# One stationary of 128 columns for V's high and low parts, in an attention and feed-forward kernel on one core

## The chip, the core and the metric

The kernel runs on one core of a Trainium2 chip. A core has a matrix engine (TensorE, PE in the profile, with its weight loads shown as PEld), a vector engine (VectorE, DVE), a scalar engine (ScalarE, ACT), a general engine (GpSimd, POOL), a queue engine (SyncE, SP) and 16 DMA engines. Matrix products land in PSUM, everything else works in SBUF. The metric is the device time of one execution in microseconds, lower is better. Before the change the median of three runs is 987.06 us (986.11 to 989.94).

## The reference

```python
# attention: B, H, S, D = 4, 8, 768, 64, 16 centroids per head, all float32
q_assign = argmax(q_n . c_n);  k_assign = argmax(k_n . c_n)      # cluster of each token
mask = q_assign[:, :, :, None] == k_assign[:, :, None, :]
scores = where(mask, q @ k.T / sqrt(D), -1e9)
attn = exp(scores - max);  attn = attn / (sum(attn) + 1e-9)
x = (attn @ v)                                  # (B, H, S, D), then to (B*S, H*D) = (3072, 512)
# feed forward: d_model 512, d_ff 2048
h = x @ w_in
g = h * tanh(softplus(h))                       # mish
out = g @ w_out
```

The result is to have float32 accuracy. The matrix engine is fed with pairs of 16-bit numbers, a high part and a low part (the rest), and products of parts are added up in PSUM.

## The kernel before

Attention is cut into 96 units: batch and head outermost (32 of them, called g), and inside each head three blocks `qb` of 256 queries. A unit has two halves `a` of 128 queries. For each half PE makes the scores (L488 and L493, float32), DVE takes the row maximum (L503), ACT the exponential (L510), POOL or DVE the reciprocal of the sum (L520, L521), POOL the high part of the normalized probabilities (L539) and DVE the low part (L556), both 16 bit; a DMA transposes both into the tile `pt`, whose 12 slices of keys are six of the high part and six of the low part (L572). This is what the units after batch 0 do. In batch 0 (units 0 to 23, where `mode` is 3) the probabilities stay float32, PE transposes them (L549), and V is float32 too.

Two units are one product with V, `pv(m)`. After batch 0 it has three parts: high of V times high of p, low of V times high of p, high of V times low of p. Each part takes six slices of 128 keys, and in each slice there is one matmul for either unit: a stationary of 64 columns (the 64 columns of the head in V), 256 columns of `pt` moving. The first unit's matmuls write partitions 0 to 63 of the PSUM tile `o`, the second unit's partitions 64 to 127, turn by turn. So there are 3 x 6 x 2 = 36 matmuls in one `pv`, and 36 such products after batch 0. Then `pv_out` takes each unit's 64 x 256 numbers out of PSUM: ACT writes the high 16-bit part of `x` (L617), DVE the low part (L618).

The feed-forward part works on blocks of 256 tokens: `m1(j)` makes 256 rows of h for one block (24 matmuls, L649 to L651), `e_mish`, `e_gh` and `e_gl` (ACT L659, POOL L663, DVE L671) make the 16-bit parts of g, `m2(k, a, f)` adds g times w_out into the tile `O` (six matmuls a step, L687 to L689), `m_out` takes it out (ACT L695). It runs some 25 units behind attention, so that PE has both kinds of work from batch 1 on. Before that the weights are converted: `w_abs`, `w_f32`, `w_sq` (L239 to L264), then `w_hi` and `w_lo` (L282 to L297) split them in two parts.

The order is not written by hand. Every step is put into a plan with a due time, in units of attention, from the table `T` (L806): for instance `m2` says how many steps after its block's first m1 a block's second product is due, `w0` when the two halves of the weights start, `prep_hi` when q and k are prepared. Fractions such as `f_a`, `f_b` and `f_w` say which share of a step's runs goes to one engine rather than another. A scheduler then orders the instructions on each engine from the plan and the dependences, and every engine works its own list in that order. Buffers come from pools (`xp` holds the tiles of `x`, `mp` small tiles of the feed-forward part), and a PSUM bank called "M" is shared by `o`, the transposed one-hots `oh` and a few scalars.

Of the kernel before, what the change touches and what calls it, by code (L numbers as in the profile page):

```python
# [8 lines left out]
F32 = mybir.dt.float32  # L9
F32R = mybir.dt.float32r  # L10
F16 = mybir.dt.float16
# [3 lines left out]
AF = mybir.ActivationFunctionType  # L15
ALU = mybir.AluOpType
AX = mybir.AxisListType

B, H, S, D, NCL = 4, 8, 768, 64, 16
DM, DFF = 512, 2048  # L20
P = 128
BIG = float(2.0**64)
E20 = 485165195.40979
PS = float(2.0**14)
# [31 lines left out]
def tile_clustered_attention_mish_ffn(  # L56
# [9 lines left out]
    nc = tc.nc  # L66
    pool = lambda name, bufs, **kw: ctx.enter_context(tc.tile_pool(name=name, bufs=bufs, **kw))
# [4 lines left out]
    op1 = pool("operands1", 1)  # L72
# [2 lines left out]
    pp = pool("probs", 3)  # L75
    hlp = pool("probs16", 3)
    ptp = pool("probsT", 3)
    xp = pool("x", 21)
    mp = pool("moe", 2)
    gp = pool("g", 1)  # L80
    sm = pool("small", 4)
# [6 lines left out]
    def share(n, key, late):  # L88

        f = T[key, int(late)]  # L90
        return int((n + 1) * f) != int(n * f)
# [24 lines left out]
    units = [(g, qb, g) for g in range(NG) for qb in range(3)]  # L116
# [89 lines left out]
    st = {}  # L206
# [93 lines left out]
    vst = {}  # L300
# [222 lines left out]
    def mode(i, a):  # L523


        n, late = 2 * i + a, i >= T["units0"]
        if i < 3 * H:
            return 3
        return 2 if share(n, "f_lo", late) else int(share(n, "f_hi", late))
# [46 lines left out]
    def pv(m):  # L576

        for i in (2 * m, 2 * m + 1):
            b, h = divmod(units[i][0], H)
            pl.after(("ptrans", i, 0), ("ptrans", i, 1), ("v_split", b, h // 2))  # L580
        o = ps2.tile([P, 512], F32, tag="M", name=f"o{m}", bufs=1)
        parts = 1 if mode(2 * m, 0) == 3 else 3
        for part in range(parts):
            for c in range(6):
                for s in range(2):
                    b, h = divmod(units[2 * m + s][0], H)
                    v = vst[b, h // 2][:, c, h % 2]
                    nc.tensor.matmul(  # L588
                        o[s * D : s * D + D, :256],
                        v if parts == 1 else v[:, int(part == 1)],  # L590
                        st["pt", 2 * m + s][:, :, c + (6 if part == 2 else 0), :],
                        start=(part == 0 and c == 0), stop=(part == parts - 1 and c == 5), skip_group_check=True,
                    )
        if parts == 1:

            for s in range(2):
                for a in range(2):
                    pl.after(("recip", 2 * m + s, a))
                    c0 = 256 + a * P
                    nc.tensor.matmul(  # L600
                        o[s * D : s * D + D, c0 : c0 + P], st["l", 2 * m + s, a].to_broadcast([P, D]), ident,
                        start=True, stop=True, skip_group_check=True,
                    )
        st["o", m] = o

    def pv_out(i):
        pl.after(("pv", i // 2))
        g, qb, _ = units[i]
        b, h = divmod(g, H)
        r, r2 = i % 2 * D, h % 2 * D  # L610
        o = st["o", i // 2][r : r + D]
        if ("x", b, h // 2, qb) not in st:
            st["x", b, h // 2, qb] = xp.tile([P, 2, 256], F16, tag="x", name=f"x{b}_{h // 2}_{qb}")
        x = st["x", b, h // 2, qb]
        if mode(i, 0) != 3:
            x = x[r2 : r2 + D]
            nc.scalar.activation(x[:, 0], o[:, :256], AF.Copy, scale=1.0 / PS)  # L617
            nc.vector.scalar_tensor_tensor(  # L618
                x[:, 1], o[:, :256], 1.0 / PS, x[:, 0], op0=ALU.mult, op1=ALU.subtract
            )  # L620
            return
        if h % 2 == 0:
            st["xf", h // 2, qb] = hlp.tile([P, 256], F32, tag="hl", name=f"xf{h // 2}_{qb}")
        xf = st["xf", h // 2, qb]
        if i % 2 == 0:
            st["rb"] = mp.tile([P, 256], F32, tag="osb", name=f"rb{i}", bufs=1)
            nc.scalar.activation(st["rb"], st["o", i // 2][:, 256:], AF.Copy, scale=vst[b, "p"])
        nc.vector.tensor_tensor(xf[r2 : r2 + D], o[:, :256], st["rb"][r : r + D], op=ALU.mult)
        if h % 2:
            nc.scalar.copy(x[:, 0], xf)  # L630
            nc.gpsimd.tensor_tensor(x[:, 1], xf, x[:, 0], op=ALU.subtract)

# [97 lines left out]
    for n in range(32):  # L730
        p = n // 16
# [5 lines left out]
    for i in range(16):  # L737
        p = i // 8
# [35 lines left out]
    for i in range(NU):  # L774
        for a in range(2):
            pl.at(i + T["scores", a], scores, i, a)
            pl.at(i + T["rowmax", a], rowmax, i, a)
            pl.at(i + T["expo", a], expo, i, a)
            pl.at(i + T["recip", a], recip, i, a)
            q = "q" if mode(i, a) == 3 else "p"  # L780
            pl.at(i + T[f"{q}_hi", a], p_hi, i, a)
            pl.at(i + T[f"{q}_lo", a], p_lo, i, a)
            pl.at(i + T[f"{q}_trans", a], ptrans, i, a)
        if i % 2:
            pl.at(i + T["pv"], pv, i // 2)
            pl.at(i + T["pv_out"], pv_out, i - 1)
            pl.at(i + T["pv_out"], pv_out, i)
# [32 lines left out]
    ('dq', 'copy_z'): 0,  # L820
    ('dq', 'copy_b'): -9,
    ('dq', 'copy_a'): 0,
    ('f_copy_t', 0): 0.269,
    ('f_copy_z', 0): 0.567,
    ('f_copy_b', 0): 0,
    ('f_copy_a', 0): 0,
# [2 lines left out]
    ('f_copy_b', 1): 0,  # L829
    ('f_copy_a', 1): 0.193,  # L830
    ('f_a', 0): 1,
    ('f_a', 1): 0.582,
    ('f_b', 0): -1,
    ('f_b', 1): 0.674,
    'prep_hi': 3.0343,
    'prep_lo': 1.2726,
    'copy_t': 0.5952,
    'copy_z': 0.8008,
    'copy_b': 3.5728,
# [13 lines left out]
    ('q_lo', 1): 1.5418,  # L853
    ('q_trans', 1): 1.5,
    ('f_w', 0): 0,
    ('f_w', 1): 0.7,
    'lead': 0.5333,
    'units0': 24,
    ('f_d', 0): 0.965,
# [10 lines left out]
    ('span', 0): 1.1575,  # L870
    ('span', 1): 1.0762,
    ('load', 0): -3.8837,
    ('load', 1): 2.8855,
    ('w0', 0): 0.89,
    ('w0', 1): 9.386,
    ('w_d', 0): 0.3597,
    ('w_d', 1): 0.1964,
    ('ws0', 0): 4.1159,
# [7 lines left out]
    'put': 2.3669,  # L886
    ('scores', 0): 0.4,
    ('rowmax', 0): 0.9821,
    ('expo', 0): 1.3834,
    ('recip', 0): 0.7,  # L890
    ('scores', 1): 1.8591,
    ('rowmax', 1): 1.6368,
# [7 lines left out]
    ('p_trans', 1): 1.5,  # L900
    'pv': 3.4,
    'pv_out': 3.6,
    'm2': 3.759,
    'm_out': 0.4,
}

# [27 lines left out]
```

## Time and profile before

| what | value |
|---|---|
| median of three runs | 987.06 us (986.11 to 989.94) |
| the profiled execution: its own time | 990.56 us |
| its span in the trace | 988.8 us |
| PE busy | 913.1 us (92%) |
| PEld busy | 660.7 us (67%) |
| DVE, ACT, POOL busy | 652.6, 542.3, 425.6 us (66, 55, 43%) |
| granted TensorE clock, mean | 0.98 of full speed |

The profiled execution is 3.5 us above the median of the runs, and 1.8 us of its time lie outside the span. Busy time of PE is the union over overlapping matmuls: a matmul's own duration is longer than its distance to the next one, so distances between starts are the measure of what one costs.

### The profile page before, as it was taken

To read this page: it belongs to the slowest core of one execution; us is meant where nothing else is said; L and a number is where in the kernel's file an instruction comes from. 1 tells how busy PE (TensorE), PEld (TensorE's weight loads), DVE (VectorE), ACT (ScalarE), POOL (GpSimd) and SP (SyncE) were. 2 spreads that over 40 slices of the span, in tenths; PEclk is the share of its full clock that TensorE was granted. 3 is DMA by queue.
4 is the path that set the end of the run, shared out by engine and by line. 5 is a ranking of instruction groups with operands and counts; after the bars stand their busy time and mean duration, and the time that the engine had idled before them with its cause. 6 is when DMAs were issued, how large, how long until landed. Compare 5 with 4: busy or idle time off the path is not lost. (4 is left out here: it accounts for less than half of the span.)

```text
span 988.8 us, 17975 instructions
## 1 busy us (share of the span) xinstructions
PE 913.1 (92%) x6913; PEld 660.7 (67%) x6913; DVE 652.6 (66%) x1149; ACT 542.3 (55%) x898; POOL 425.6 (43%) x539
## 2 busy tenths in 40 slices
PE   3898688998998999999999999899999999999997
PEld 3666466676666766766777767667777777676764
DVE  6988985877867776867767777767776766211110
ACT  3777374775656666476656747556556565211111
POOL 3225785626535444653544544744444433111010
PEclk9999788999999999999999999999999999999999
DMA  9734623136785776667678766667667656100000
GB/s 360 238 78 149 183 60 69 45 79 130 132 158 97 163 126 115 134 142 152 122 147 144 149 135 127 125 131 139 132 114 136 120 106 115 43 12 22 12 11 22
DMA packets 250165, 115.50 MB, mean 117 GB/s; under 512 B 229600, under 2 KB 229600, under 8 KB 250080
## 3 DMA queue, kind: packets, MB, share of 16 engines
q1 hardware_dynamic: 238272, 82.50, 42.3%
q10 hardware_dynamic: 11808, 31.86, 11.4%
q8 instruction: 54, 0.88, 0.4%
q14 instruction: 31, 0.25, 0.1%
HBM read 35.68 MB, written 6.29 MB: 42 GB/s over the span
## 5 line engine op out<-in xcount | busy, mean ns | idle before, releaser
L510 ACT ACTIVATE p<-s,m 128x768 f32<-128x768 f32 x192 | 172.7, 900 | 161.3 <-DVE m L503 123.3
L649 PE MATMUL h<-x,w 128*128 128x256 f16 x768 | 210.0, 273 | 2.7 <-ACT u L659 1.8
L650 PE MATMUL h<-x,w 128*128 128x256 f16 x768 | 209.6, 273 | 0.3 <-DVE x L618 0.3
L651 PE MATMUL h<-x,w 128*128 128x256 f16 x768 | 209.6, 273 | 0.0
L556 DVE SCALAR_TENSOR_TENSOR hl<-p,l,hl 128x768 f16<-128x768 f32 x144 | 162.1, 1129 | 65.9 <-POOL hl L539 65.4
L539 POOL TENSOR_SCALAR hl<-p,l 128x768 f16<-128x768 f32 x144 | 133.1, 926 | 126.9 <-DVE l L521 51.4
L503 DVE TENSOR_REDUCE m<-s 128x1 f32<-128x768 f32 x192 | 181.0, 947 | 5.4 <-PE s L493 4.0
L671 DVE SCALAR_TENSOR_TENSOR g<-u,mscg,g 128x512 f16<-128x512 f32 x96 | 79.7, 833 | 137.7 <-POOL g L663 136.9
L663 POOL TENSOR_SCALAR g<-u,mscg 128x512 f16<-128x512 f32 x96 | 78.9, 823 | 180.7 <-ACT u L659 151.8
L687 PE MATMUL O<-w,g 128*128 128x512 f16 x384 | 146.1, 381 | 4.8 <-POOL g L663 4.0
L689 PE MATMUL O<-w,g 128*128 128x512 f16 x384 | 145.7, 379 | 1.4 <-DVE g L671 0.9
L688 PE MATMUL O<-w,g 128*128 128x512 f16 x384 | 145.6, 379 | 0.0
L488 PE MATMUL s<-A,B 128*128 128x384 f32 x384 | 122.9, 402 | 21.4 <-ACT p L510 18.3
L659 ACT ACTIVATE u<-h,msch 128x512 f32<-128x512 f32 x96 | 65.3, 686 | 98.5 <-PE h L651 96.8
L520 POOL TENSOR_SCALAR l<-l 128x1 f32<-128x1 f32 x129 | 39.7, 308 | 160.4 <-ACT p L510 156.9
L493 PE MATMUL s<-Z,T 80*128 80x384 f32 x384 | 101.2, 345 | 4.5 <-ACT T L467 2.4
L488 PEld LDWEIGHTS s<-A,B 128*128 128x128 f32 x384 | 63.5, 193 | 45.8 <-ACT p L510 26.2
L649 PEld LDWEIGHTS <-w 128*128 128x128 f16 x768 | 75.2, 98 | 22.6 <-issue 8.1
L650 PEld LDWEIGHTS <-w 128*128 128x128 f16 x768 | 75.3, 98 | 19.9 <-issue 5.1
L651 PEld LDWEIGHTS <-w 128*128 128x128 f16 x768 | 75.2, 98 | 14.5 <-issue 4.1
L588 PE MATMUL o<-pt,v 128*64 128x256 f16 x1296 | 81.4, 274 | 0.1
L588 PEld LDWEIGHTS <-v 128*64 128x64 f16 x1296 | 68.0, 110 | 15.8 <-issue 12.8
(185 smaller groups left out, 1314.9 us busy)
## 6 DMA issues: line engine op xcount, KB each, us to landing
qk<-in_qk_dram ACTq DMA_DIRECT2D x32, 384.0 KB, 4.0
stage<-in_w_out_dram ACTq DMA_DIRECT2D x16, 512.0 KB, 4.5
vraw<-in_vP_dram SPq DMA_DIRECT2D x16, 384.0 KB, 4.0
out_dram<-osb SPq DMA_DIRECT2D x24, 256.0 KB, 2.3
B<-T ACTq DMA_DIRECT2D x30, 192.0 KB, 4.1
A<-A SPq DMA_DIRECT2D x25, 192.0 KB, 4.7
stage<-in_w_in_dram SPq DMA_DIRECT2D x8, 512.0 KB, 8.9
stage<-in_w_in_dram ACTq DMA_DIRECT2D x8, 512.0 KB, 4.1
```

The source lines that it names most:

```text
L488: nc.tensor.matmul(s[:, j, :384], st["B", n][:, q0 : q0 + P], st["A", n][:, j * 384 : (j + 1) * 384], start=True, stop=False,)
L503: nc.vector.tensor_reduce(m, st["s", i, a][:, :, :384], axis=AX.XY, op=ALU.max, negate=True)
L510: in_turn(nc.scalar.activation(p.rearrange("p (n x) -> p n x", n=2), st["s", i, a][:, :, :384], AF.Exp, bias=st["m", i, a], scale=1.0, acc ...
L539: nc.gpsimd.tensor_scalar(t[:, 0], p, r, 1.0, op0=ALU.mult, op1=ALU.mult)
L556: nc.vector.scalar_tensor_tensor(t[:, 1], p, r, t[:, 0], op0=ALU.mult, op1=ALU.subtract)
L588: nc.tensor.matmul(o[s * D : s * D + D, :256], v if parts == 1 else v[:, int(part == 1)], st["pt", 2 * m + s][:, :, c + (6 if part == 2 el ...
L649: nc.tensor.matmul(o, wh, xh, start=(c == 0), stop=False)
L650: nc.tensor.matmul(o, wh, xl, start=False, stop=False)
L651: nc.tensor.matmul(o, wl, xh, start=False, stop=(c == 3))
L687: nc.tensor.matmul(o, gh, wh, start=(f == 0 and fi == 0), stop=False)
L688: nc.tensor.matmul(o, gh, wl, start=False, stop=False)
L689: nc.tensor.matmul(o, gl, wh, start=False, stop=(f == 7 and fi == 1))
```

## The change

After batch 0 the product with V takes the high and the low part of V side by side as one stationary of 128 columns. Partitions 0 to 63 of `o` then collect the high part of V, 64 to 127 the low part, and the two units stand in the two halves of its 512 columns. The moving side runs through all 12 slices of `pt`, so the product of both low parts, left out before, is computed as well. `pv_out` takes the low half of `o` to a float32 tile `xf` (ACT), adds the high half to it (DVE), and when both heads of a tile are there, ACT writes the high 16-bit part of `x` and POOL the low part, as batch 0 did before.

```diff
-        parts = 1 if mode(2 * m, 0) == 3 else 3
-        for part in range(parts):
...
-                        o[s * D : s * D + D, :256],
-                        v if parts == 1 else v[:, int(part == 1)],
-                        st["pt", 2 * m + s][:, :, c + (6 if part == 2 else 0), :],
...
+            for s in range(2):
+                b, h = divmod(units[2 * m + s][0], H)
+                for c in range(6):
+                    for part in range(2):
+                        nc.tensor.matmul(
+                            o[:, s * 256 : s * 256 + 256], vst[b, h // 2][:, c, h % 2].rearrange("p g d -> p (g d)"),
+                            st["pt", 2 * m + s][:, :, c + 6 * part, :],
...
-            nc.scalar.activation(x[:, 0], o[:, :256], AF.Copy, scale=1.0 / PS)
-            nc.vector.scalar_tensor_tensor(
-                x[:, 1], o[:, :256], 1.0 / PS, x[:, 0], op0=ALU.mult, op1=ALU.subtract
-            )
...
+            nc.scalar.activation(xh, o[D:], AF.Copy, scale=1.0 / PS)
+            nc.vector.scalar_tensor_tensor(xh, o[:D], 1.0 / PS, xh, op0=ALU.mult, op1=ALU.add)
         if h % 2:
+            x = st["x", b, h // 2, qb] = xp.tile([P, 2, 256], F16, tag="x", name=f"x{b}_{h // 2}_{qb}")
             nc.scalar.copy(x[:, 0], xf)
             nc.gpsimd.tensor_tensor(x[:, 1], xf, x[:, 0], op=ALU.subtract)
...
-    'm2': 3.759,
+    'm2': 4.327,
```

Nine numbers of the table move with it. In the program as built they come to this: `m2` is due 0.57 steps later; the second half of the weights starts 0.51 units later (`w0`); of the preparations of q and k 16 go from a scaling and a subtraction on POOL to one instruction on DVE (24 to 8 on POOL, 8 to 24 on DVE), and their high parts A go from 22 on POOL and 10 on ACT to 14 and 18; of the second weights' splits three go from DVE to POOL, and two of their scalings from ACT to POOL; two copies of T go from ACT to a DMA. `xf` gets three buffers in `mp`, and `xp` has 18 instead of 21.

On PE the first place is a product with V in the middle of the run. `v` is the split V, `pt` the transposed probabilities of either unit, `O` the product before it, `s` the scores behind it. The list before:

```order
L689 MATMUL O_1_7623<-w_1272,g_7490 128x512
L588 LDWEIGHTS v_0_7377
L588 MATMUL o_7947<-pt_7609,v_0_7377 64x256
L588 LDWEIGHTS v_0_7377
L588 MATMUL o_7947<-pt_7688,v_0_7377 64x256
L588 LDWEIGHTS v_0_7377
L588 MATMUL o_7947<-pt_7609,v_0_7377 64x256
L488 MATMUL s_1_7926<-A_7574,B_7598 128x384 x2
L493 MATMUL s_1_7926<-Z_7600,T_7577 128x384 x2
L588 LDWEIGHTS v_0_7377
```

The list of the changed kernel at a like place:

```order
L695 MATMUL O_1_7452<-w_1251,g_7129 128x512
L598 LDWEIGHTS v_0_7156
L598 MATMUL o_7715<-pt_7384,v_0_7156 128x256
L598 LDWEIGHTS v_0_7156
L598 MATMUL o_7715<-pt_7384,v_0_7156 128x256
L598 LDWEIGHTS v_0_7156
L598 MATMUL o_7715<-pt_7384,v_0_7156 128x256
L598 LDWEIGHTS v_0_7156
```

The pairs of 64-column matmuls, one from each unit, have become single ones of 128 columns that stay with one unit; each still has its own weight load, though two that follow each other use the same part of V. Before, the scheduler put scores between some of the pairs.

On ACT the second place is the way from `o` to `x`, in batch 2, for the two units that complete the second pair of heads. Before:

```order
L510 ACTIVATE p_0_6462,l_0_6463<-s_0_6416,m_0_6460 128x768
L617 ACTIVATE x_1_1_6018<-o_6379 64x256
L617 ACTIVATE x_1_2_6240<-o_6379 64x256
L396 CAST T_6552<-A_6549 64x768
L510 ACTIVATE p_1_6502,l_1_6503<-s_1_6495,m_1_6500 128x768
```

In the changed kernel:

```order
L510 ACTIVATE p_0_6288,l_0_6289<-s_0_6235,m_0_6286 128x768
L632 ACTIVATE xf_1_1_5859<-o_6210 64x256
L636 CAST x_1_1_6278<-xf_1_1_5859 128x256
L632 ACTIVATE xf_1_2_6069<-o_6210 64x256
L378 ACTIVATE A_6375<-qk_6312,scq 128x768
L636 CAST x_1_2_6283<-xf_1_2_6069 128x256
L396 CAST T_6377<-A_6375 64x768
L510 ACTIVATE p_1_6328,l_1_6329<-s_1_6321,m_1_6326 128x768
```

Two casts and one high part A now stand between two exponentials where only the two takings-out and a copy stood.

On PE the third place is the end of the last m1 (`h`) and the m2 steps (`O`, from `g`) around it. Before:

```order
L649 MATMUL h_11203<-x_3_2_10160,w_693 128x256
L687 LDWEIGHTS g_11192
L687 MATMUL O_0_11068<-w_1272,g_11192 128x512
L688 LDWEIGHTS g_11192
L688 MATMUL O_0_11068<-w_1272,g_11192 128x512
L650 LDWEIGHTS w_693
L650 MATMUL h_11203<-x_3_2_10160,w_693 128x256
L651 LDWEIGHTS w_693
L651 MATMUL h_11203<-x_3_2_10160,w_693 128x256
L689 LDWEIGHTS g_11192
```

In the changed kernel:

```order
L656 MATMUL h_10855<-x_3_2_9951,w_691 128x256
L657 LDWEIGHTS w_691
L657 MATMUL h_10855<-x_3_2_9951,w_691 128x256
L693 LDWEIGHTS g_10880
L693 MATMUL O_0_10756<-w_1314,g_10880 128x512
L694 LDWEIGHTS g_10880
L694 MATMUL O_0_10756<-w_1314,g_10880 128x512
L695 LDWEIGHTS g_10880
```

Before, two of the six matmuls of the last step but one of m2 stood ahead of the last two of m1; now the whole step stands behind it, ahead of the step that needs the last g.

## Rows read from the trace of the kernel before

**Rows 1.** Three stretches and 100 to 120: busy us by engine, granted clock

```profile
core 0: us, PE busy (x) PEld busy (x) DVE busy (x) ACT busy (x) POOL busy (x), PEclk, DMA share, GB/s
0.00:240.00 240.00, 191.92 (x1362) 147.43 (x1363) 193.43 (x385) 146.68 (x278) 123.58 (x165) 0.92 0.47 137
100.00:120.00 20.00, 14.23 (x100) 10.04 (x101) 19.87 (x24) 5.29 (x10) 16.48 (x12) 0.84 0.61 185
240.00:855.00 615.00, 592.87 (x4694) 429.50 (x4695) 440.69 (x741) 374.65 (x590) 286.16 (x352) 1.00 0.68 131
855.00:988.00 133.00, 128.34 (x861) 83.77 (x858) 18.50 (x25) 20.99 (x31) 15.86 (x23) 1.00 0.04 15
```

**Rows 2.** Waits of PE after 240 us: total us, times, longest

```profile
PE s L488 <- ACT p L510: 9.8, 15, 1.3
PE O L687 <- POOL g L663: 4.0, 5, 1.2
...
PE O L689 <- DVE g L671: 0.9, 3, 0.5
```

**Rows 3.** Timeline of PE: start, us, line, operation, shape, count

```profile
505.29 0.38 PE L689 MATMUL O<-w,g 128*128 128x512 f16 x1
...
506.21 0.39 PE L687 MATMUL O<-w,g 128*128 128x512 f16 x1
...
507.30 0.38 PE L689 MATMUL O<-w,g 128*128 128x512 f16 x1
507.61 2.15 PE L588 MATMUL o<-pt,v 128*64 128x256 f16 x36
509.69 0.62 PE L488 MATMUL s<-A,B 128*128 128x384 f32 x2
...
510.50 0.28 PE L649 MATMUL h<-x,w 128*128 128x256 f16 x1
...
510.74 0.27 PE L651 MATMUL h<-x,w 128*128 128x256 f16 x1
...
513.03 0.27 PE L651 MATMUL h<-x,w 128*128 128x256 f16 x1
```

**Rows 4.** The same view, a product with V between 16-bit steps

```profile
438.92 0.38 PE L688 MATMUL O<-w,g 128*128 128x512 f16 x1
439.14 0.38 PE L689 MATMUL O<-w,g 128*128 128x512 f16 x1
439.45 2.16 PE L588 MATMUL o<-pt,v 128*64 128x256 f16 x36
441.53 0.39 PE L687 MATMUL O<-w,g 128*128 128x512 f16 x1
441.76 0.38 PE L688 MATMUL O<-w,g 128*128 128x512 f16 x1
```

**Rows 5.** Groups by line and shape: busy us, mean ns, idle before

```profile
L384 POOL TENSOR_TENSOR B<-qk,A 128x768 fp32r<-128x768 f32 x24 | 45.0, 1875 | 2.0 <-ACT A L378 1.0
...
L631 POOL TENSOR_TENSOR x<-xf,x 128x256 f16<-128x256 f32 x12 | 8.6, 726 | 5.2 <-ACT x L630 5.0
L386 DVE SCALAR_TENSOR_TENSOR B<-qk,scq,A 128x768 fp32r<-128x768 f32 x8 | 8.1, 1007 | 0.0
...
L295 DVE SCALAR_TENSOR_TENSOR w<-w,ws1r,w 128x1024 f16<-128x1024 f32 x5 | 7.4, 1472 | 0.0
...
L630 ACT CAST x<-xf 128x256 f16<-128x256 f32 x12 | 4.9, 406 | 4.5 <-DVE xf L628 4.3
```

**Rows 6.** Waits of ACT, 240 to 855 us

```profile
ACT x L617 <- DVE x L618: 49.8, 28, 5.2
```

**Rows 7.** Timeline of PE at the end, idle time in brackets

```profile
971.88 0.39 PE L687 MATMUL O<-w,g 128*128 128x512 f16 x1 [0.70 <-POOL g L663]
```

**Rows 8.** Waits of PE in the first 240 us

```profile
PE gram L264 <- DVE w L249: 10.0, 10, 2.4
PE s L488 <- ACT p L510: 9.6, 11, 2.4
```

More of the change, by code (lines that the diff above doesn't have):

```diff
@@ L77, in tile_clustered_attention_mish_ffn @@
     ptp = pool("probsT", 3)
-    xp = pool("x", 21)
+    xp = pool("x", 18)
     mp = pool("moe", 2)
@@ L581, in pv @@
         o = ps2.tile([P, 512], F32, tag="M", name=f"o{m}", bufs=1)
-        parts = 1 if mode(2 * m, 0) == 3 else 3
-        for part in range(parts):
+        early = mode(2 * m, 0) == 3
+        if early:
             for c in range(6):
@@ L586, in pv @@
                     b, h = divmod(units[2 * m + s][0], H)
-                    v = vst[b, h // 2][:, c, h % 2]
                     nc.tensor.matmul(
-                        o[s * D : s * D + D, :256],
-                        v if parts == 1 else v[:, int(part == 1)],
-                        st["pt", 2 * m + s][:, :, c + (6 if part == 2 else 0), :],
-                        start=(part == 0 and c == 0), stop=(part == parts - 1 and c == 5), skip_group_check=True,
-                    )
-        if parts == 1:
+                        o[s * D : s * D + D, :256], vst[b, h // 2][:, c, h % 2], st["pt", 2 * m + s][:, :, c, :],
+                        start=(c == 0), stop=(c == 5), skip_group_check=True,
+                    )
+        else:
+            for s in range(2):
[5 more added lines that the diff above has]
+                            st["pt", 2 * m + s][:, :, c + 6 * part, :],
+                            start=(part == 0 and c == 0), stop=(part == 1 and c == 5), skip_group_check=True,
+                        )
+        if early:
             for s in range(2):
@@ L610, in pv_out @@
         r, r2 = i % 2 * D, h % 2 * D
[L611 to L616, printed above, removed]
-            nc.scalar.activation(x[:, 0], o[:, :256], AF.Copy, scale=1.0 / PS)
-            nc.vector.scalar_tensor_tensor(
-                x[:, 1], o[:, :256], 1.0 / PS, x[:, 0], op0=ALU.mult, op1=ALU.subtract
-            )
-            return
+        o = st["o", i // 2]
         if h % 2 == 0:
-            st["xf", h // 2, qb] = hlp.tile([P, 256], F32, tag="hl", name=f"xf{h // 2}_{qb}")
+            st["xf", h // 2, qb] = mp.tile([P, 256], F32, tag="xf", name=f"xf{b}_{h // 2}_{qb}", bufs=3)
         xf = st["xf", h // 2, qb]
[L625 to L628, printed above, removed]
+        xh = xf[r2 : r2 + D]
+        if mode(i, 0) == 3:
+            if i % 2 == 0:
+                st["rb"] = mp.tile([P, 256], F32, tag="osb", name=f"rb{i}", bufs=1)
+                nc.scalar.activation(st["rb"], o[:, 256:], AF.Copy, scale=vst[b, "p"])
+            nc.vector.tensor_tensor(xh, o[r : r + D, :256], st["rb"][r : r + D], op=ALU.mult)
+        else:
+            o = o[:, i % 2 * 256 : i % 2 * 256 + 256]
+            nc.scalar.activation(xh, o[D:], AF.Copy, scale=1.0 / PS)
+            nc.vector.scalar_tensor_tensor(xh, o[:D], 1.0 / PS, xh, op0=ALU.mult, op1=ALU.add)
         if h % 2:
+            x = st["x", b, h // 2, qb] = xp.tile([P, 2, 256], F16, tag="x", name=f"x{b}_{h // 2}_{qb}")
             nc.scalar.copy(x[:, 0], xf)
@@ L822 @@
     ('dq', 'copy_a'): 0,
-    ('f_copy_t', 0): 0.269,
+    ('f_copy_t', 0): 0,
     ('f_copy_z', 0): 0.567,
@@ L831 @@
     ('f_a', 0): 1,
-    ('f_a', 1): 0.582,
+    ('f_a', 1): 0.239,
     ('f_b', 0): -1,
-    ('f_b', 1): 0.674,
+    ('f_b', 1): 0,
     'prep_hi': 3.0343,
-    'prep_lo': 1.2726,
+    'prep_lo': 1.1321,
     'copy_t': 0.5952,
@@ L855 @@
     ('f_w', 0): 0,
-    ('f_w', 1): 0.7,
+    ('f_w', 1): 0.363,
     'lead': 0.5333,
@@ L872 @@
     ('load', 0): -3.8837,
-    ('load', 1): 2.8855,
+    ('load', 1): 2.8849,
     ('w0', 0): 0.89,
-    ('w0', 1): 9.386,
+    ('w0', 1): 9.896,
     ('w_d', 0): 0.3597,
@@ L888 @@
     ('rowmax', 0): 0.9821,
-    ('expo', 0): 1.3834,
+    ('expo', 0): 2.0645,
     ('recip', 0): 0.7,
```

## The prediction

> **What bounds the kernel now.** I read first the busy time by stretch, then what PE waits for, then the timeline of PE around single products with V. From 240 to 855 us, where attention of batches 1 to 3 runs beside the feed-forward part, PE is busy 592.87 of 615 us at the full granted clock, while DVE has 440.69 and ACT 374.65 [rows 1]. After 855 only the feed-forward part is left, and PE is busy 128.34 of 133. What stops PE from 240 us to the end is little: 9.8 us of scores that wait for an exponential to free their PSUM tile, 4.0 and 0.9 us of m2 that waits for g, and a few smaller ones [rows 2]. So in this stretch PE's own list sets the time, and what the change adds to or takes from that list comes out nearly whole. The first 240 us are different: PE is busy 191.92 and the clock is 0.92 on average, and DVE is as busy with 193.43 (from 100 to 120 it has 19.87 of 20) [rows 1].
>
> **The product with V on PE.** This is the term that decides. The timeline merges the 36 matmuls of one product into one row of 2.15 us [rows 3]. The last of them takes 0.27 by itself, as its 256-column neighbours do, so the first and the last pair start 1.88 apart. These are 17 steps from pair to pair, 0.111 us each, and 18 pairs make 1.99 us. A pair, that is two matmuls on 64 columns each, takes as long as one matmul on 128 columns: in m1, with the same 128 x 128 stationary and 256 columns moving that the change brings, two rows 21 matmuls apart lie 2.29 us apart, 0.109 each [rows 3]. So the two halves of the array do run at the same time, and the kernel before pays for 18 full matmuls in a product where the changed one pays for 24. Each of the 24 has its own weight load as in m1, where the load is hidden. 24 x 0.109 = 2.62 us. Over 36 products that is 36 x (2.62 - 1.99) = +22.7 us.
>
> Against this stands what going into and out of the half-array form costs. Take scores alone: from the start of the m2 matmul before them to the next 16-bit matmul behind them it is 505.29 to 506.21, 0.92 us. With a product with V ahead of the scores it is 507.30 to 510.50, 3.20 us [rows 3]. So the product costs 2.28 us and not 1.99; 0.29 is lost at its two ends. Between two 16-bit steps it is 439.14 to 441.76, 2.62 us, where two m2 matmuls at 0.22 would take 0.44 [rows 4]: the product costs 2.18 there, 0.19 lost. The changed product has the form of m1, and m1 shows no such loss at its ends. In the whole timeline of PE the 36 products stand in 51 pieces, since the scheduler puts other work between pairs; 29 pieces end at float32 work (scores, assignments) and 22 at 16-bit work. That is 29 x 0.29 + 22 x 0.19 = 12.6 us that goes. Net: 22.7 - 12.6 = +10.1 us on an engine with no room. The bounds of this term: +22.7 if as much is lost at the ends of the new form, for a reason of its own, and +10.1 if nothing is; I take +10.1, since m2 passes into scores and back in the rows at 0.92 less 0.22, 0.70 us, which is the nearest row.
>
> One rule of the Trainium skill speaks against the change: "TensorEngine Tiling (Array Packing)", Theoretical Speedup and When to Use Tiling, gives up to two times for a stationary of at most 64 columns when it is put on half the columns. By this rule alone the change undoes a factor of two on work that it cuts by a third, which is the +22.7. The same page says under Key Properties that a change of the tiling mode drains the engine, without a price; the trace agrees with 0.19 to 0.29 us for the two ends of a piece, and by both rules together the sum is the +10.1.
>
> **The waits of m2 for g.** m2 is due 0.57 steps later, so that between a block's g and its use more of other work lies on PE. The last m2 shows it: now PE idles 0.70 us for POOL's part of the last g [rows 7], and in the changed order a whole step of six matmuls (six of 0.22, 1.3 us) is in between. All waits of this kind after 240 us make 4.9 us [rows 2]. Bounds: 0 (g comes as late again) and -4.9; I take the middle, -2.5. m2 that is later keeps its g buffers longer, but their next user stands behind further m1 work in the plan, so I charge nothing for it.
>
> **From o to x.** The two takings-out stay what they were, one on ACT and one on DVE for each of 72 units. New are 36 casts on ACT at 0.406 and 36 subtractions on POOL at 0.726 [rows 5], 14.6 and 26.1 us. POOL has room (286.16 of 615) and loses more than that: 16 subtractions of 1.875, 30 us, and their scalings. DVE gets the 16 as 1.007 each and loses three of 1.472: +11.7 us. ACT gets eight more high parts of q and k as well, of 768 columns, three times a cast's: at most 1.2 each, an estimate from the cast's 0.406, so 24 us with the casts, 4% of the stretch; it is at 374.65 of 615. These hide beside PE as long as PE's lists meet no late partner. The place where it can show is ACT's order: a cast waits for DVE's addition, and behind it stand exponentials that free the PSUM tile for scores. Already ACT waits 49.8 us in 28 places for DVE's part of x before it may take out the next unit, 1.8 each [rows 6]. With 36 such waits more, ACT's list could lose up to 36 x (0.4 + 1.8) = 80 us of its 240 idle ones. What of it reaches PE is the 9.8 us row. Bounds: the row doubles, +9.8; or it shrinks by a third, -3, since POOL, which makes the high part of p, has less in its way. I take +1.
>
> **The first 240 us.** The second half of the weights starts 0.51 units later, and its 18 or so conversions on DVE at units 10 to 14 come in two smaller heaps. DVE's work there stays the same to 1.4 us (three splits fewer, 4.4, and some three preparations more, 3.0). PE waits there 10.0 us for the weights' conversions, since their small squares stand in its list [rows 8]. Bounds: -10.0, and +5 (half of it once more); I take -1, because an engine that is full from 100 to 120 us does not get emptier by an order that shifts its heap. The three fewer buffers of x cost nothing: x is now allocated at the second head of a pair, three units later than before.
>
> **The sum.** +10.1 - 2.5 + 1 - 1 = +7.6 us. The profiled execution took 990.56 us, so a like one would take 998.2; it lies 3.5 above the median of the runs, 987.06, and the same sum on the median gives 994.7.
>
> **The rivals.** (1) The ends are lost all the same, or the moving side of `pt` in 128-column form runs slower than m1's: the full +22.7, with -2.5 for g: 1007. For it speaks only that no such product is in the trace; against it m1's shape. (2) The way to x holds up ACT: 10.1 - 2.5 + 9.8 = +17.4, 1004.5. For it speak the 49.8 us; against it that the changed order has 18 matmuls of m1 and four of m2 more, 2.8 us, between the last product with V that batch 1's first m1 needs and the point where it needs it. (3) PE's waits shrink as much as its work grows: all 4.9 for g and half of the 9.8 for exponentials go, +10.1 - 9.8 = 0, 987.4: no change. For it speaks that every other engine gains 0.3 us a product while PE works; against it that these waits were few already. (4) Faster: the first 240 us give back the 10.0 us of the weights' conversions and half of the 9.6 for exponentials [rows 8], and m2 its 4.9: 10.1 - 10.0 - 4.8 - 4.9 = -9.6, 977.5. It decides from 15.1 us given back by waits (10.1 plus the 5 that count as faster). For it speaks that PE idles 48 us there; against it that DVE's work stays. That the change does not do what it says is excluded by its order: 36 products of 24 matmuls.
>
> **How the numbers follow.** The forecast, 989 to 1000 us, gets 0.47; (1) 0.09, (2) 0.12, (3) 0.17, (4) 0.15. 0.5% of 987.06 is 4.9 us, about what a measurement of this kernel can tell from no change: below 982.1 is faster, above 992.0 slower. Faster: 0.15, from (4). Within: 0.17 of (3) and 0.15 of the forecast's lower end, 0.32. Slower: the forecast's other 0.32 with (1) and (2), 0.53. The range of 8 in 10 leaves out (4) and a half of (1): 982 to 1007. The likeliest case's own range is 989 to 1000.
>
> **What would show it.** In the changed profile the product with V should be one row of 24 matmuls on 128 columns, some 2.8 us long in the timeline (23 x 0.109 and one of 0.27), with 0.11 from its last start to a 16-bit neighbour, and scores behind it should take 0.70 us as behind m2. If the row is longer than 2.9 or its ends cost 0.2, (1) is right. PE's waits for exponentials after 240 us should stay near 10 us; 20 would be (2), 5 would be (3). The idle time of PE before the first product with 16-bit V should stay near 48 us; under 35 would be (4). I am wrong if the time is below 989 with the ends of the products gone as foreseen: then waits decide here, and not PE's list.

## The result and the profile after

The changed kernel takes 978.73 us (median of 4 runs, 978.06 to 980.81); the kernel before, on the same chip in the same comparison, 988.5 us (4 runs, 986.11 to 991.98). The ratio is 0.9897, with a 95% interval of 0.9876 to 0.9918: some 10 us faster, where 994.7, slower, was forecast. The time lies below the range of 982 to 1007 as well. The profiled execution took 978.06 us with a span of 976.3; that of before 990.56 with 988.8.

First the three stretches, as in [rows 1], with the same columns; the last ends where this span ends:

```profile
0.00:240.00 240.00, 199.16 (x1416) 153.63 (x1417) 200.23 (x398) 153.11 (x288) 129.58 (x174) 0.93 0.52 145
240.00:855.00 615.00, 602.93 (x4295) 447.37 (x4293) 428.25 (x744) 390.59 (x624) 266.38 (x350) 1.00 0.67 129
855.00:976.00 121.00, 116.40 (x775) 75.29 (x772) 16.43 (x21) 18.55 (x27) 14.03 (x21) 1.00 0.04 16
```

PE is busy 602.93 of the middle 615 us, where it was 592.87: its idle time there went from 22.1 to 12.1 us. In the first 240 us it went from 48 to 41. ACT does 16 us more in the middle stretch, as it had to; DVE does 12 us less, though more work was put on it.

Next PE's waits, total us, times and longest. After 240 us, the view of [rows 2]:

```profile
PE s L488 <- ACT p L510: 8.1, 8, 2.1
PE O L693 <- POOL g L669: 2.1, 3, 1.0
...
PE O L695 <- DVE g L677: 0.4, 2, 0.2
```

In the first 240 us, the view of [rows 8]:

```profile
PE gram L264 <- DVE w L249: 14.7, 9, 3.7
...
PE s L488 <- ACT p L510: 4.6, 6, 1.7
```

After 240 us the waits for exponentials are 8.1 (from 9.8), those of m2 for g 2.5 (from 4.9). In the first 240 the waits for the weights' conversions grew from 10.0 to 14.7, while those for exponentials halved, from 9.6 to 4.6. These rows stand for some of the lost time only: PE's view counts a wait from the end of the matmul before it, and a matmul's own duration is longer than the usual distance to the next start (0.27 against 0.109 us in m1). Weight loads have a view of their own. PEld's waits for exponentials after 240 us, before:

```profile
PEld s L488 <- ACT p L510: 14.9, 18, 1.6
```

and in the changed kernel:

```profile
PEld s L488 <- ACT p L510: 11.7, 12, 2.4
```

For the most part these are the same waits seen from an earlier start, and not further ones: of the 9.8 us of PE's row before, all but 0.1 lie inside these 14.9.

Last the product with V in PE's timeline (start, us, line, shape, count), in the surroundings of the second half of [rows 3]:

```profile
509.69 0.38 PE L695 MATMUL O<-w,g 128*128 128x512 f16 x1
509.90 2.78 PE L598 MATMUL o<-pt,v 128*128 128x256 f16 x24
512.44 0.60 PE L488 MATMUL s<-A,B 128*128 128x384 f32 x2
512.88 0.51 PE L493 MATMUL s<-Z,T 80*128 80x384 f32 x2
513.23 0.28 PE L655 MATMUL h<-x,w 128*128 128x256 f16 x1
```

The product is one row of 24 matmuls, 2.78 us. From the m2 matmul ahead of it to the m1 behind the scores it is 509.69 to 513.23, 3.54 us; the scores alone took 0.92 [rows 3], so the product costs 2.62, as worked out, and nothing at its ends. From 512.44 to 513.23 the scores take 0.79, against 0.81 behind the old product and 0.70 foreseen.

To split PE's time into its list and its waits without either wait view, I added up, from the first m1 on, the usual distance from start to start of each matmul, by its kind and the kind before it (the lower quartile over all kernels profiled here). This is the list; what is left of the time from the first m1 to the last matmul is waits. In us of the one profiled execution of each kernel:

```
kernel        first m1   list    waits   total
before          215.1    727.5    42.1   769.5
after           208.2    736.9    27.2   764.1
v_alone         215.0    736.4    38.9   775.3
v_m2            212.5    736.3    33.1   769.5
table_alone     207.2    726.8    32.4   759.2
early_alone     208.5    730.4    40.8   771.2
late_alone      212.9    727.5    33.8   761.3
prep_alone      209.6    729.9    35.7   765.6
way_table       208.2    727.9    30.6   758.5
half_p          208.3    689.7    48.8   738.5
```

The levels depend on how finely the kinds are told apart: other ways put the waits of before at 42 to 50 us. The differences between kernels move by up to 2 us with it. PE's gaps in the trace from the first m1 on, the part of the waits that its busy time leaves open, are 26.6 us before, 14.3 after and 30.3 in half_p.

So the list grew by 9.4 us, where 10.1 was worked out; the waits fell by 14.9, and the first m1 starts 6.9 earlier: 9.4 - 14.9 - 6.9 = -12.4 us between the two profiles. Such single profiles lie up to 4.3 us from the medians of their kernels, so what follows goes by the ratios of runs, and by this table for the direction only.

### The profile page after: what moved, and what is told of

It reads as the page before. It is cut to its first block, busy times and chain, and to the rows that moved or that the text cites. A ratio compares the mean times of both kernels' runs of the same rounds, so it can differ in the third digit from the quotient of the medians.

```text
span 976.3 us, 17239 instructions
## 1 busy us (share of the span) xinstructions
PE 918.5 (94%) x6481; PEld 676.3 (69%) x6481; DVE 644.9 (66%) x1162; ACT 562.2 (58%) x938; POOL 410.0 (42%) x543
## 5 line engine op out<-in xcount | busy, mean ns | idle before, releaser
L556 DVE SCALAR_TENSOR_TENSOR hl<-p,l,hl 128x768 f16<-128x768 f32 x144 | 152.3, 1058 | 72.7 <-POOL hl L539 72.4
L539 POOL TENSOR_SCALAR hl<-p,l 128x768 f16<-128x768 f32 x144 | 132.7, 922 | 125.2 <-ACT p L510 47.5
L677 DVE SCALAR_TENSOR_TENSOR g<-u,mscg,g 128x512 f16<-128x512 f32 x96 | 75.8, 792 | 139.8 <-POOL g L669 139.0
L488 PE MATMUL s<-A,B 128*128 128x384 f32 x384 | 123.3, 402 | 14.9 <-ACT p L510 12.7
L598 PE MATMUL o<-pt,v 128*128 128x256 f16 x864 | 102.7, 273 | 0.6 <-DMA pt<-hl 0.4
L520 POOL TENSOR_SCALAR l<-l 128x1 f32<-128x1 f32 x129 | 40.5, 314 | 142.7 <-ACT p L510 139.5
L598 PEld LDWEIGHTS <-v 128*128 128x128 f16 x864 | 83.8, 98 | 16.6 <-issue 1.7
L488 PEld LDWEIGHTS s<-A,B 128*128 128x128 f32 x384 | 64.1, 194 | 33.5 <-ACT p L510 18.5
```

The lines of the kernel that those rows point to most:

```text
L488: nc.tensor.matmul(s[:, j, :384], st["B", n][:, q0 : q0 + P], st["A", n][:, j * 384 : (j + 1) * 384], start=True, stop=False,)
L539: nc.gpsimd.tensor_scalar(t[:, 0], p, r, 1.0, op0=ALU.mult, op1=ALU.mult)
L556: nc.vector.scalar_tensor_tensor(t[:, 1], p, r, t[:, 0], op0=ALU.mult, op1=ALU.subtract)
L598: nc.tensor.matmul(o[:, s * 256 : s * 256 + 256], vst[b, h // 2][:, c, h % 2].rearrange("p g d -> p (g d)"), st["pt", 2 * m + s][:, :, c + ...
```

## The experiments

The change is a new form of product, a new way from `o` to `x`, and nine numbers of the table. The theory formed on the result (T) was that the table's moves give the gain and that the product costs time, as forecast but less. "Before" is 988.9 to 989.8 us in these comparisons; ratios carry their 95% interval.

**The new product and way, with the table of before (v_alone).**

```diff
+            for s in range(2):  # the product and pv_out as in the change
...
     'm2': 3.759,  # and the other eight numbers as before
```

> The changed product with V and the changed way to x (with 18 buffers of x), but all nine numbers of the table as before. Theory T (the table's order of the first 240 us gives the gain, the product itself costs): PE's list grows by some 10 us from 240 us on and little is given back, so slower than before by 4 to 12 us, 992 to 1000 us, with the first product with 16-bit V at about 231 us as before. Rival R (the product itself gives the gain, by ends that are no longer lost and by waits that vanish with it; the table is neutral): 977 to 983 us.

Measured: 993.23 us, 1.0050 [1.0032, 1.0067]. The change of form by itself makes the kernel slower by 4.9 us: the sign of the forecast for the form (+10.1 for the product and +1 for the way), at about half its size.

**The whole table, with the product and way of before (table_alone).**

```diff
-    'm2': 3.759,
+    'm2': 4.327,
...
-    ('w0', 1): 9.386,
+    ('w0', 1): 9.896,
```

> The product with V and the way to x as before, all nine numbers of the table as in the changed kernel. Theory T: the early gain without the product's cost: 970 to 979 us, the first product with 16-bit V near 222 us. Rival R: 985 to 991 us, as before.

Measured: 971.61 us, 0.9824 [0.9805, 0.9843]. This version is faster than both kernels: by 17.4 us than before, and by 0.74% (0.9897 / 0.9824) than the changed one. The gain is the table's, and the new form costs 7.2 us on top of it.

**The early numbers alone (early_alone):** the start of the weights' second half, the engines of the second weights' splits, and the copies of T.

```diff
-    ('f_copy_t', 0): 0.269,
+    ('f_copy_t', 0): 0,
...
-    ('f_w', 1): 0.7,
+    ('f_w', 1): 0.363,
...
-    ('w0', 1): 9.386,
+    ('w0', 1): 9.896,
```

> The kernel before with only the three numbers that act in the first 240 us changed: w0 (second weights 0.51 units later), f_w (three splits from DVE to POOL, two scalings from ACT to POOL) and f_copy_t (two copies of T by DMA). Theory T: nearly the whole early gain, 8 to 12 us faster than before, 976 to 981 us. Rival R: 985 to 991 us.

Measured: 982.52 us, 0.9939 [0.9920, 0.9958], 6 us of the 17.4 and less than the 8 to 12 that theory T expected.

**The late numbers alone (late_alone):** where preparations run, and m2's delay. The other three of these numbers change the order of no engine.

```diff
-    ('f_a', 1): 0.582,
-    ('f_b', 1): 0.674,
+    ('f_a', 1): 0.239,
+    ('f_b', 1): 0,
...
-    'm2': 3.759,
+    'm2': 4.327,
```

> The kernel before with only the numbers that act later changed: m2 0.57 steps later, and the preparations of q and k after batch 0 taken from POOL to DVE and ACT (f_a, f_b), with three numbers that should change no order (prep_lo, load, expo). Theory T: 2 to 6 us faster than before from fewer waits after 240 us, 982 to 987 us, and the first product with 16-bit V not before 229 us. Rival R: 985 to 991 us.

Measured: 979.14 us, 0.9903 [0.9885, 0.9921]: 9.6 us, more than the early ones, and more than expected. Together the halves make 15.6 of 17.4.

**m2's delay alone (m2_alone).**

```diff
-    'm2': 3.759,
+    'm2': 4.327,
```

> The kernel before with m2 due 0.57 steps later and nothing else. Theory M (the later gain of the table is m2's: its steps no longer meet a g that is late, and they cut into m1 less often): 5 to 9 us faster than before, 980 to 984 us, and PE's idle time after the first m1 down from 42 us to some 35. Rival P (the later gain comes from POOL's relief, the preparations of q and k taken to DVE and ACT): 986 to 990 us, idle time as before.

Measured: 989.27 us, 1.0002 [0.9987, 1.0017]. Alone it gives nothing, so the theory that m2 makes the late gain falls.

**The preparations alone (prep_alone).** 16 of them go from POOL to DVE, and eight high parts A from POOL to ACT.

```diff
-    ('f_a', 1): 0.582,
-    ('f_b', 1): 0.674,
+    ('f_a', 1): 0.239,
+    ('f_b', 1): 0,
```

> The kernel before with the preparations of q and k after batch 0 taken from POOL to DVE and ACT (f_a, f_b), m2 as before. Theory M: within 2 us of before, 987 to 991 us. Rival P: 5 to 9 us faster, 980 to 984 us, with POOL's part of the probabilities and the exponentials behind it earlier and fewer scores waiting for ACT.

Measured: 985.53 us, 0.9957 [0.9935, 0.9978]. That is 4.3 us; less than rival P expected. With m2's nothing it does not make late_alone's 9.6: 5 us are left, uncertain by some 3. The two edits work together, and by which wait is open.

**The start of the weights' second half alone (w0_alone).**

```diff
-    ('w0', 1): 9.386,
+    ('w0', 1): 9.896,
```

> The kernel before with the second half of the weights 0.51 units later and nothing else. Theory W (the early gain is w0's: the heap of conversions on DVE at units 10 to 14 is cut in two): 4 to 7 us faster than before, 982 to 985 us, scores of unit 36 some 6 us earlier. Rival F (it is the three splits taken from DVE to POOL): 987 to 991 us.

Measured: 983.77 us, 0.9943 [0.9925, 0.9961], as theory W expected.

**The splits of the second weights alone (fw_alone).**

```diff
-    ('f_w', 1): 0.7,
+    ('f_w', 1): 0.363,
```

> The kernel before with f_w changed alone: three of the second weights' splits from DVE to POOL, two scalings from ACT to POOL. Theory W: within 2 us of before, 987 to 991 us. Rival F: 4 to 7 us faster, 982 to 985 us, since DVE, which is full there, loses 4.4 us.

Measured: 985.29 us, 0.9961 [0.9944, 0.9978], near what rival F expected, so neither theory holds alone. With the splits three high parts of the weights go from ACT to POOL as well (L288, 11 before and 14 here). The two early edits give 5.6 and 3.9 alone, and with the copies of T 6.0 together: it seems that they take away much of the same loss. In the table above the early ones bring the first m1 6.6 us forward and leave the waits behind it alone (42.1 to 40.8).

**The way from o to x alone, old product and old table (way_alone).** The old `o` holds 64 rows, so the same half is taken out by ACT and added by DVE, each with half the scale; the instructions and their sizes are those of the change.

```diff
-            nc.scalar.activation(x[:, 0], o[:, :256], AF.Copy, scale=1.0 / PS)
+            nc.scalar.activation(xh, o[:, :256], AF.Copy, scale=0.5 / PS)
+            nc.vector.scalar_tensor_tensor(xh, o[:, :256], 0.5 / PS, xh, op0=ALU.mult, op1=ALU.add)
...
-    xp = pool("x", 21)
+    xp = pool("x", 18)
```

> The kernel before with only the new way from o to x: the 36 matmuls of 64 columns stay, ACT writes half of o to the float32 tile xf, DVE adds the other half, ACT casts and POOL subtracts, so the same instructions and sizes as in the changed kernel (18 buffers of x). Old table. Theory T (V's part is slower by its PE work alone): 0 to 2 us over before, 988 to 992 us. Rival X (its cost is the way to x, by which ACT waits longer): 4 to 6 us over before, 993 to 996 us, as slow as with the new product.

Measured: 994.39 us, 1.0041 [1.0023, 1.0060]. The way, with its 18 buffers of x, costs 4.1 us, which is nearly all that v_alone lost. The longer product, by division 1.0050 / 1.0041, costs 0.9 us here, uncertain by some 2.5 (both intervals together): not the 9 us by which PE's list is longer. PE's gaps from the first m1 on are 29.2 us in way_alone and 22.5 in v_alone: some 7 of the 9 us stand where gaps were.

**The same way with the new table (way_table).**

```diff
+            nc.scalar.activation(xh, o[:, :256], AF.Copy, scale=0.5 / PS)  # as way_alone
...
+    'm2': 4.327,  # and the other eight numbers as in the change
```

> The same with the whole new table: only the product with V differs from the changed kernel. Theory T: the time of the new table with the old product and the old way, 970 to 974 us, so that the new product alone costs 5 to 9 us, near the 9 us by which PE's list is longer. Rival X: 977 to 981 us, the time of the changed kernel.

Measured: 974.74 us, 0.9846 [0.9818, 0.9874]. With the new table the way costs 2.2 us (0.9846 / 0.9824) and the longer product 0.52% (0.9897 / 0.9846), 5 us, each uncertain by some 3.5. That lies between what theory T and rival X expected. The product seems again to cost less than the 9 us of its list. Whether it costs more here, with fewer waits beside it, than with the old table, these intervals don't tell.

**Half the product (half_p).** This is the changed kernel without the product with the low part of p: 12 of 24 matmuls are left out, and the result lacks that part. All other instructions stay, but the scheduler orders some of them anew: on DVE 307 of 1162 places, and on ACT 93 of 938, hold an instruction on other tiles than in the changed kernel.

```diff
-                    for part in range(2):
+                    for part in range(1):
...
-                            start=(part == 0 and c == 0), stop=(part == 1 and c == 5), skip_group_check=True,
+                            start=(c == 0), stop=(c == 5), skip_group_check=True,
```

> The changed kernel without the low part of the probabilities in the product with V: 12 of its 24 matmuls left out, everything else as it was (the result lacks that part). It takes 36 x 12 x 0.109 = 47 us from PE's list. Theory T (PE's list sets the time, waits take a little back): 40 to 47 us faster than the changed kernel, 932 to 939 us. Rival Y (from the first m1 on, chains through DVE and ACT set the time, and PE's list hides under them): 20 to 30 us faster at most, 949 to 959 us, with PE's idle time after the first m1 up by the rest.

Measured: 953.67 us, 0.9641 [0.9605, 0.9677]. Against the changed kernel's 0.9897 that is 25 us (uncertain by 4), as rival Y expected, while PE's list lost 36 x 12 x 0.109 = 47.1 us (47.2 in the table above). PE's waits after 240 us in this kernel:

```profile
PE s L488 <- ACT p L510: 13.1, 14, 2.6
PE h L655 <- ACT u L665: 5.2, 6, 1.5
```

and those of its weight loads:

```profile
PEld s L488 <- ACT p L510: 21.8, 26, 2.9
```

Scores wait 13.1 us for exponentials (8.1 in the changed kernel; 21.8 and 11.7 as their weight loads show the same waits), and m1 now waits 5.2 for ACT. Of the 47.2 us taken from the list, 21.6 come back as waits (27.2 to 48.8).

**The new product and way with m2 alone of the table (v_m2).**

```diff
-    'm2': 3.759,
+    'm2': 4.327,  # the other eight numbers as before; product and pv_out as in the change
```

> The changed product with V and way to x, with m2 as in the changed kernel and the other eight numbers of the table as before. Theory N (m2's delay is worth nothing by itself, with the old product or the new one): as the product alone with the old table, 992 to 996 us. Rival O (m2's delay goes with the new product): 986 to 989 us.

Measured: 987.93 us, 0.9975 [0.9957, 0.9993]. m2's delay, worth nothing on the old kernel, is worth 0.75% beside the new product (0.9975 / 1.0050), 7.4 us (uncertain by some 2.5), as rival O expected. As beside the moved preparations, it shows its worth only together with another edit; through which wait is not shown.

## Why the prediction was wrong

**Two steps failed.** The larger one is what the sum gave the table: -2.5 for m2's waits, -1 for the first 240 us and nothing of their own for the preparations, -3.5 in all. table_alone measures -17.4. That alone turns the sign: with -17.4 in its place the rest of the sum gives 10.1 + 1 - 17.4 = -6.3.

The other is the one drawn from the bounds: that from 240 us on "what the change adds to or takes from that list comes out nearly whole". The sign of being wrong that the prediction gives for it, a time below 989 with the ends of the products gone, is there, but the table alone would have given it as well; half_p tests the step apart: it takes 47.2 us from the list and gains 25, a little over half. way_alone against v_alone adds about 9 us to it and loses 1; with the new table the same product loses 5, uncertain as said. An engine busy 96% of a stretch still had some 42 us of waits behind the first m1. The PE rows that I read showed 14.7 [rows 2]; that view's rows add up to 24.2, PE's gaps from the first m1 on to 26.6, and the starts to 42. The argument against rival (3), that "these waits were few already", rested on the 14.7. The same bound hid the table's gain: table_alone leaves the list as it was (727.5 and 726.8) and takes 9.7 us from the waits. That other engines catch up while PE works longer, and are late while it works less, fits the wait rows of half_p; what part of it comes from the scheduler's other order is not shown.

**The product's own cost was right.** 24 x 0.109 foreseen as 2.62, measured 2.62; the ends are gone as foreseen, the list grew 9.4 for 10.1. By the Trainium skill, "TensorEngine Tiling (Array Packing)", Key Properties, a change of tiling mode drains the engine; the trace of after agrees, since the 0.29 us at two ends is no longer there in the 3.54. But a right sum over a list is not a time.

**The table's moves were the larger half of the change, and I sized them near nothing.** I gave the first 240 us -1, "because an engine that is full from 100 to 120 us does not get emptier by an order that shifts its heap". early_alone gives -6.0, beyond the -1 and inside the bounds of -10 to +5. DVE did not get emptier: from 100 to 120 us it has 19.89 of 20 in early_alone, and 19.87 before. What fell are waits of attention. PE's waits from 100 us to the first m1, before (100 to 215):

```profile
PE gram L264 <- DVE w L249: 9.1, 8, 2.4
PE s L488 <- ACT p L510: 3.5, 6, 1.4
```

and in early_alone (100 to 208):

```profile
PE gram L264 <- DVE w L249: 9.9, 6, 3.5
...
PE s L488 <- ACT p L510: 0.3, 1, 0.3
```

The waits for the weights' conversions stay, those of scores nearly vanish, and those of batch 0's transposes (L549) go from 6.4 to 2.5. The rows of first m1 show it on PE, before:

```profile
215.08 0.27 PE L649 MATMUL h<-x,w 128*128 128x256 f16 x1
```

and in the changed kernel:

```profile
208.18 0.28 PE L655 MATMUL h<-x,w 128*128 128x256 f16 x1
```

v_alone's first m1 stands at 215.03 and early_alone's at 208.51. So this part is the early numbers' work, and not the product's.

**The preparations that leave POOL** I costed at nothing ("these hide beside PE"). They give 4.3 us alone, and 9.6 with m2. Foreseen was +11.7 us on DVE; measured is 652.6 to 644.9 over the whole span, 7.7 less, and 645.5 with the preparations alone. The groups of DVE (busy us, mean ns of one) show most of it. Before:

```profile
L556 DVE SCALAR_TENSOR_TENSOR hl<-p,l,hl 128x768 f16<-128x768 f32 x144 | 162.1, 1129 | 65.9 <-POOL hl L539 65.4
...
L456 DVE TENSOR_TENSOR onehot<-D,Dm 128x192 bf16<-128x192 f32 x32 | 27.0, 845 | 0.7
```

In the changed kernel, with the preparations that were moved:

```profile
L556 DVE SCALAR_TENSOR_TENSOR hl<-p,l,hl 128x768 f16<-128x768 f32 x144 | 152.3, 1058 | 72.7 <-POOL hl L539 72.4
...
L386 DVE SCALAR_TENSOR_TENSOR B<-qk,scq,A 128x768 fp32r<-128x768 f32 x24 | 26.6, 1110 | 0.2
...
L456 DVE TENSOR_TENSOR onehot<-D,Dm 128x192 bf16<-128x192 f32 x32 | 16.5, 517 | 0.5
```

And with the preparations moved alone (prep_alone):

```profile
L556 DVE SCALAR_TENSOR_TENSOR hl<-p,l,hl 128x768 f16<-128x768 f32 x144 | 153.3, 1067 | 64.9 <-POOL hl L539 64.4
...
L456 DVE TENSOR_TENSOR onehot<-D,Dm 128x192 bf16<-128x192 f32 x32 | 16.3, 508 | 0.5
```

The 24 preparations on DVE cost 26.6 us, 18.5 more than the eight before, where 16.1 was foreseen. But two groups that the change doesn't touch take less: DVE's 144 splits of p 9.8 us, and its 32 one-hot comparisons (L456) 10.5. m2_alone leaves their means at 1135 and 922 ns. DVE's part of g fell too, from 833 to 792 ns, but it stays at 830 with the preparations alone, so that is not their work. What the shorter groups share is in the section on the hardware; how DVE's relief reaches PE is not shown.

**m2's waits** for g fell by 2.4 us (4.9 to 2.5), as foreseen with 2.5. That this would show as time by itself was wrong: in m2_alone the waits for POOL's part of g fall as well (4.0 to 2.2 after 240 us), and the ratio is 1.0002. Its last wait behaves as argued (0.70 in [rows 7]):

```profile
959.50 0.39 PE L693 MATMUL O<-w,g 128*128 128x512 f16 x1 [0.27 <-POOL g L669]
```

**The way from o to x** had +1, with bounds of -3 and +9.8. It costs 4.1 us alone and 2.2, uncertain by 3.5, with the new table: a term inside its bounds, of the kind that rival (2) names, and mis-sized by 1 to 3 us. ACT's waits for DVE on this way, the view of [rows 6], are now two rows:

```profile
ACT x L636 <- DVE xf L633: 24.4, 18, 2.6
ACT xf L632 <- DVE xf L633: 23.1, 19, 2.3
```

Their sum is 47.5 us, where it was 49.8: the casts wait 24.4 us in 18 places, but the takings-out wait for half of what they did. The 80 us feared of ACT's list did not come.

**The rivals.** (1) is out: the ends are gone. (2) is real at 2.2 to 4.1 of its 9.8 us: in way_alone scores wait 13.3 us for exponentials after 240 us, 9.8 before. (3) named waits that shrink as work grows. Where only the product is added (way_table to the changed kernel), the table above has 3.4 us fewer waits for 9.0 more of list. Of the 14.9 us of waits that went in all, 9.7 go with the table alone, where the list does not grow. (4) gave 977.5, near the 978.73, with half of its mechanism: in the first 240 us the waits for exponentials fell by 5.0 where it said 4.8, and those for g by 2.4 where it said 4.9. But the waits for the weights' conversions, which it let vanish, grew from 10.0 to 14.7, PE's idle time before the first product with 16-bit V is 40.3 (47.0 before) and not under 35, and the preparations have no part in it. That its time comes so near is luck in part. By the ratios, the sum that should have stood there is -17.4 for the table and +7.2 for the new form: the way +2.2 and the product +5.

**What stays open:** why m2's delay pays only beside the moved preparations or the new product. The runs show that it does, twice; no run takes the waits apart. Open too is how much of half_p's lost gain is the scheduler's other order. The sum of list and waits shows the direction (v_alone 38.9 us of waits, v_m2 33.1), not which partner came earlier.

## What to carry to other kernels

Before a row "busy 96%" is taken as "every microsecond of work counts", add up the engine's list from the usual distances of start to start and see what is left; here it was 42 us, where PE's gaps were 26.6 and the rows read 14.7. Rows of weight loads show waits of their matmuls over again and are not added to them. Where an order is planned by a table, split the edit: here the 9 us that a product added to a full engine cost 1 to 5, and the numbers that came with it were worth 17. When the parts are known, run the best of them together: here the old product with the new table, 971.61 us.

## What the runs showed of the hardware

Some elementwise instructions on DVE take longer while POOL works on a large tile. The clearest is the one-hot comparison, 128 x 192, which the change leaves alone. In the trace of before it stands once beside a subtraction of a preparation on POOL:

```profile
82.13 1.83 POOL L384 TENSOR_TENSOR B<-qk,A 128x768 fp32r<-128x768 f32 x1
...
82.69 1.48 DVE L456 TENSOR_TENSOR onehot<-D,Dm 128x192 bf16<-128x192 f32 x1
```

and once with no work on POOL beside it:

```profile
451.39 0.36 DVE L456 TENSOR_TENSOR onehot<-D,Dm 128x192 bf16<-128x192 f32 x1
```

The five of the 32 that no POOL instruction overlaps take 0.354 us in the mean. The 14 that overlap such a subtraction longest take 1.279; in the changed kernel there are four of that kind, at 1.052, and 17 that stand alone, at 0.352. DVE's split of p, 128 x 768 in float32, stands in the timeline of before beside one of POOL's scalings:

```profile
336.34 0.91 POOL L373 TENSOR_SCALAR qk<-qk,scq 128x768 f32<-128x768 f32 x1
336.40 1.65 DVE L556 SCALAR_TENSOR_TENSOR hl<-p,l,hl 128x768 f16<-128x768 f32 x1 [1.10 <-POOL hl L539]
```

and in the changed kernel at a place without such a scaling:

```profile
307.55 1.02 DVE L556 SCALAR_TENSOR_TENSOR hl<-p,l,hl 128x768 f16<-128x768 f32 x1 [0.63 <-POOL hl L539]
```

It is 1.65 us against 1.02. In the trace of before, 11 of the 144 splits have a scaling of L373 as the POOL instruction that they overlap longest, and their mean is 1.505 us; the 53 that no POOL instruction overlaps have 1.016, and the 30 beside POOL's 128 x 1 work on the sums (L520) 1.021. In the changed kernel there is none beside a scaling. These 11 make 5.4 of the 9.8 us. All this is seen side by side in the traces and was not measured by itself. But work that moves from POOL to DVE can cost DVE less than its own duration: with the preparations moved alone, DVE does 16.4 us more of them and is busy 7.1 us less in all.
